# Linear attention, expert routing and a gated MLP on one core: loads from two queues, score products in one group, a separate tile for token ids

## The chip, the core and the metric

The kernel runs on one core of a Trainium2 chip. The core has a matrix engine (PE, TensorE; its weight loads are shown as PEld), two elementwise engines (DVE, VectorE, and ACT, ScalarE), a general engine (POOL, GpSimd) and an engine that only issues transfers (SP, SyncE). ACT and POOL can issue transfers too; an instruction that issues one stands in its engine's own stream and waits there for its semaphores. Sixteen DMA engines move the data. The metric is the time of one execution in microseconds; a run's time is compared as a median.

## The reference

Three stages follow each other. `B, H, S, D = 4, 8, 768, 48`, so there are 3072 tokens of 384 features.

```
f = sigmoid(f_logit)
for t in range(S):
    state = f[:, :, t, :, None] * state + outer(k[:, :, t], v[:, :, t])
    y[:, :, t] = q[:, :, t] @ state
x = y as (3072, 384)
expert_idx = argmax(normalized(x) @ normalized(expert_emb).T / tau); gate_w = softmax value of it
x[mask_e] = gate_w * (relu(x[mask_e] @ w1[e]) @ w2[e])          # 8 experts, 384 -> 1024 -> 384
out = ((x @ w_a) * (x @ w_b)) @ w_out                            # 384 -> 1536 -> 384
```

## The kernel before

**Attention (L119 to L619).** The sequence is cut into 24 groups `g` (6 chunks of 128 tokens, 4 batches each, `B` = 4). For each group `load_a` (L168) brings q, k and the gate logits (`qkf`, two halves of 48 partitions, 288 KB each; the partition rows between them are zeroed by a load of `zgap`), and `load_b` (L175) brings v in two layouts (`vx`, `vT`). `prep_f` (L183) makes the gate on ACT, `prep_s` (L189) makes on DVE a running product and its inverse by two scans and from them the tiles `kt` and `qc`. The function `pe(g)` (L303) is one round of PE: score products `pp` of group g+2 (`p_part`, L246, four parts), the products of group g with the state (`inter`) and with its masked scores (`intra`), the key-value part of group g+1 (`kv_part`), and the state update (`u_part`). PE also multiplies constants (`warm_up`, L298, tile `wp`): 22 before the first round, 5, 4 and 2 in the rounds, 24 at the end. `NKEEP` (L47) gives 4 for rounds 0 to 3 and 2 for rounds 4 to 22. `evac` (L334) takes a group's result to `yx` (8 buffers). A `route` generator, advanced by `tick` between the other DVE instructions, computes the expert, the gate and the slot of each token; `scale_row` (L427) writes the gated rows and the token's number into `xr` (3 buffers), and `scatter_row` sends them to the table `slots` in DRAM, by an indirect transfer that POOL issues.

**Experts (L622 to L878).** 64 steps `s` (8 experts, 8 slices of the hidden width). For each expert `rows_load` (L728) brings up to 448 token rows into the one tile `rows`; `x_turn` transposes them (PE, `pt`) in steps 3 to 5 of the expert before; `h_mm` and `y_part` are the products. `ids_store` (L738) writes the token numbers, column `DM` of `rows`, to `idlist` in DRAM, and the next `rows_load` follows it on SP and overwrites `rows`. The weights come through two `raw` buffers and are split into two parts by ACT, POOL and DVE (`job_load` L653, `job_run` L666).

**Gated MLP (L881 to L972).** 72 steps of products; the results are scattered to the output by the ids.

The order of each engine's instructions is the order of the Python code: nothing reorders them. A transfer from SP or ACT takes one of eight completion semaphores (DMAHW0 to DMAHW7 below), shared by both queues; it waits until the transfer that held that semaphore before has landed. `bufs` of a tile says how many buffers it goes round.

Of the kernel before, what the change touches and what calls it, by code (L numbers as in the profile page):

```python
# [6 lines left out]
F32 = mybir.dt.float32  # L7
# [3 lines left out]
ACTF = mybir.ActivationFunctionType  # L11
# [5 lines left out]
B, H, S, D = 4, 8, 768, 48  # L17
NT, DM, NE, FF, FF2 = B * S, H * D, 8, 1024, 1536
L = 128
NCH = S // L  # L20
NP = H // 2
HP = 112
QP = 128
VW = D + NE
KC = DM // 128
CAP = 448
RW = 388
# [16 lines left out]
NWARM2 = 0  # L44
NWARM3 = 24
ZR = 192
NKEEP = (4, 2)  # L47


def build(tc, I, out, dbg=None):  # L50
    nc = tc.nc
    V, A, T, G, SP = nc.vector, nc.scalar, nc.tensor, nc.gpsimd, nc.sync
# [66 lines left out]
    with tc.manual_schedule():  # L119
# [4 lines left out]
        ob_p = actx.enter_context(tc.tile_pool(name="ob", bufs=1))  # L124
        x_p = actx.enter_context(tc.tile_pool(name="x", bufs=12))
# [7 lines left out]
        NG = NCH * B  # L133
# [8 lines left out]
        en_bd = ob_p.tile([128, KC, H * NE], F32, name="en_bd")  # L142
# [6 lines left out]
        qkf_t = [ob_p.tile([QP, 3, NP, L], F32, name=f"qkf{i}") for i in range(5)]  # L149
# [18 lines left out]
        def load_a(g):  # L168
            if g < NG:
                qkf = qkf_t[g % 5]  # L170
                for i in range(2):
                    SP.dma_start(out=qkf[64 * i:64 * i + D], in_=I["qkf"][g, i])
                st[g] = dict(qkf=qkf)

        def load_b(g):  # L175
            if g < NG:
                vx = in_p.tile([128, H, VW], F32, tag="vx", name="vx", bufs=4)
                SP.dma_start(out=vx, in_=I["vx"][g])
                vT = in_p.tile([128, KC, L], F32, tag="vT", name="vT")
                SP.dma_start(out=vT, in_=I["vT"][g])  # L180
                st[g].update(vx=vx, vT=vT)
# [60 lines left out]
        def p_open(g):  # L242
            if g < NG:
                st[g]["ps"] = [ps_p.tile([128, NP, L], F32, tag="pp", name="pp") for i in range(2)]

        def p_part(g, p):  # L246
            if g >= NG:
                return
            d = st[g]
            for i in range(2):  # L250
                r = slice(64 * i, 64 * i + 64)
                T.matmul(out=d["ps"][i][:, p], lhsT=d["kt"][r, p], rhs=d["qc"][r, p], start=True, stop=True)
# [36 lines left out]
        def intra(g, ps):  # L289
            if g < 0:  # L290
                return
            d = st[g]
            for p in ps:
                for i in range(2):
                    T.matmul(out=d["y"][:, 2 * p + i], lhsT=d["pm"][i][:, p], rhs=d["vx"][:, 2 * p + i],
                             start=(g < B and p == 0 and i == 0), stop=True, skip_group_check=True)

        def warm_up(n):  # L298
            wp = ps_kv.tile([128, 512], F32, tag="kv", name="wp")
            for i in range(n):  # L300
                T.matmul(out=wp, lhsT=ones, rhs=warm, start=(i == 0), stop=(i == n - 1))

        def pe(g):  # L303
            n = g + 2
            if 0 <= g < NG - 1:
                warm_up(NKEEP[g >= B])
            p_open(n)
            p_part(n, 0)
            if g == -1:
                warm_up(NWARM1)  # L310
            p_part(n, 1)
            p_part(n, 2)
            inter(g)
            intra(g, (0,))
            p_part(n, 3)
            kv_part(g + 1)
            it[0] += 0.5
            tick(2)
            p_mask(n)
            intra(g, (1, 2, 3))  # L320
            u_part(g)
            return st.pop(g)["y"] if g >= 0 else None
# [10 lines left out]

        def evac(g, y, rd):  # L334
            i = len(rd["x"])
            yx = x_p.tile([128, H, VW], F32, tag="yx", name="yx", bufs=8)
            A.activation(out=yx, in_=y, func=ACTF.Copy)
            junk = x_p.tile([128, H, D], BF16, tag="junk", name="junk", bufs=1)
            A.activation(out=junk, in_=yx[:, :, 0:D], func=ACTF.Square, accum_out=rd["ssq"][:, i:i + 1])
            late.append(lambda: V.tensor_reduce(out=rd["lg"][:, i], in_=yx[:, :, D:VW].rearrange("p h e -> p e h"),  # L340
                                                axis=AX.X, op=ALU.add))
            rd["x"].append((g, yx))
# [82 lines left out]
        scq, scaled = [], []  # L425

        def scale_row():  # L427
            if scq:
                if len(scaled) == 3:
                    scatter_row()  # L430
                g, yx, gate, posi = scq.pop(0)
                xr = x_p.tile([128, RW], F32, tag="xr", name="xr", bufs=3)
                c, b = divmod(g, B)
                G.iota(out=xr[:, DM:RW], pattern=[[0, RW - DM]], base=b * S + c * L, channel_multiplier=1,
                       allow_small_or_imprecise_dtypes=True)
                A.activation(out=xr[:, 0:DM].rearrange("p (h e) -> p h e", h=H), in_=yx[:, :, 0:D], func=ACTF.Copy,
                             scale=gate)
                scaled.append((xr, posi))
# [35 lines left out]
                    except StopIteration:  # L474
                        bg.pop(0)

        for i in range(5):
            for r in (48, 112):
                SP.dma_start(out=qkf_t[i][r:r + 16], in_=I["zgap"].rearrange("p (a b c) -> p a b c", a=3, b=NP))
            if i < 2:  # L480
                load_a(i)
            if i == 0:
                SP.dma_start(out=en_bd, in_=I["embbd"])
                tau = ob_p.tile([128, 1], F32, name="tau")
                SP.dma_start(out=tau, in_=I["tau"].to_broadcast([128, 1]))
                load_b(0)
        V.memset(half, 0.5)
        V.memset(ones, 1.0)
        V.memset(warm, 0.0)
        A.activation(out=half, in_=half, func=ACTF.Tanh, scale=0.0, bias=0.0)  # L490
        V.memset(half, 0.5)
        onesf = raw0[:, 512:640]
# [22 lines left out]
        prep_s(0)  # L515
        V.tensor_reduce(out=en, in_=pe_ps.rearrange("p h e -> p e h"), axis=AX.X, op=ALU.add)
        G.tensor_tensor(out=en, in0=en, in1=half, op=ALU.pow)
        load_a(2)
        load_b(1)
        load_a(3)  # L520
        load_b(2)
        load_a(4)
        prep_f(2)
        prep_s(1)
        V.tensor_scalar(out=en, in0=en, scalar1=1e-6, scalar2=tau, op0=ALU.add, op1=ALU.mult)
# [98 lines left out]
        ectx = ExitStack()  # L624
        ap = ectx.enter_context(tc.tile_pool(name="acts", bufs=4))
        hp = ectx.enter_context(tc.tile_pool(name="hid", bufs=2))
        sp = ectx.enter_context(tc.tile_pool(name="solo", bufs=1))
        yT = [sp.tile([128, NT + CAP], F32, name=f"yT{k}") for k in range(KC)]
        rows = sp.tile([128, 4, RW], F32, name="rows")
        idr = sp.tile([24, 128], F32, name="idr")  # L630
# [107 lines left out]
        def ids_store(e):  # L738
            if e == 0:
                dst = idlist[0, 0:CAP]  # L740
            else:
                rs = SP.value_load(off_i[0:1, e:e + 1], **off_range(e))  # L742
                dst = idlist[0, bass.ds(rs, CAP)]
            SP.dma_start(out=dst.rearrange("(p j) -> p j", j=4), in_=rows[0:HP, :, DM])

        def x_turn(e, k):
            if e >= NE:
# [104 lines left out]
        for s in range(NE * FJ):  # L852
            e, j = divmod(s, FJ)
# [13 lines left out]
            if s == IDS + 4:  # L867
# [5 lines left out]
                ids = sp.tile([128, NT // 128], F32, name="ids")  # L873
# [300 lines left out]
```

## Time and profile before

| what | value |
|---|---|
| runs, us | 935.67, 937.55, 947.85 (median 937.55) |
| the profiled execution, us | 946.78, with a span of 945.1 from first to last instruction |
| mean granted clock of PE | 0.967 of 2.4 GHz |
| busy: PE, PEld, DVE, ACT, POOL | 95%, 83%, 44%, 36%, 24% of the span |

The profile is one execution. Times in its rows are microseconds from the first instruction unless marked ns. A matrix product of 32-bit operands shows as two records, so a group of six products reads x12. Ends of products are modelled, and neighbours overlap, so lengths are best taken from start to start. The granted clock is 1.00 at 2.4 GHz and 0.50 at 1.2 GHz. Attention lies from 0 to about 212 us, the experts from 217 to about 480, the gated MLP behind that.

### The profile page before, as it was taken

What the parts mean: (1) busy time and instruction counts of PE and PEld (TensorE: products, weight loads), DVE (VectorE), ACT (ScalarE), POOL (GpSimd) and SP (SyncE); (2) the same over time, 40 slices, a digit from 0 to 9 for tenths busy, and PEclk for the clock granted to TensorE, in tenths of its full rate; (3) what the DMA queues carried; (4) which work ended last, traced back from release to release, by engine and by line L of the source; (5) the groups of instructions that cost most, each with busy time, mean ns of one, the idle gap of its engine ahead of it and who ended that gap; (6) DMA issues with size and microseconds to landing.
All of it is one profiled execution on the core that took longest, in us unless ns stands there. A gap on an engine that the chain in (4) does not pass through costs nothing.

```text
span 945.1 us, 12533 instructions
## 1 busy us (share of the span) xinstructions
PE 895.5 (95%) x4908; PEld 781.4 (83%) x4931; DVE 417.0 (44%) x789; ACT 336.1 (36%) x601; POOL 226.7 (24%) x221
## 2 busy tenths in 40 slices
PE   5999999968989998999999899999999999999996
PEld 2788888847978897898988788888888888888885
DVE  5577787742434442343678852222322322222222
ACT  2365666533444353344434421212212222122221
POOL 2123344556253353354222211001001001001001
PEclk8599999979999999999999999999999999999999
DMA  9777877324254545535533300000000000000001
GB/s 177 184 198 197 212 201 190 124 110 126 69 157 115 138 146 146 146 102 163 102 101 101 101 1 34 0 1 34 1 1 34 1 1 34 0 1 34 1 1 37
DMA packets 42806, 83.15 MB, mean 88 GB/s; under 512 B 7532, under 2 KB 24900, under 8 KB 42740
## 3 DMA queue, kind: packets, MB, share of 16 engines
q1 hardware_dynamic: 39668, 72.78, 29.4%
q0 software_dynamic: 3072, 9.49, 2.8%
q8 instruction: 41, 0.67, 0.3%
q14 instruction: 25, 0.20, 0.1%
HBM read 70.36 MB, written 11.90 MB: 87 GB/s over the span
## 4 chain that ended last, share of the span: by engine, by line
issue 48%; DMA 12%; POOL 7%; PE 5%; SPq 1%; DVE 1%; POOLq 0%; ACT 0%; DVEq 0%; ACTq 0%
DMA idlist<-rows 5%; DMA raw<-moe_w 5%; POOL w L672 3%; PE po L812 2%; POOL w L690 2%; POOL out L937 2%; DMA rows<-slots 1%; PE ph L759 1%; PE ph L760 1%; PE ph L761 1%; SPq L742 0%; SPq L663 0%; PE pt L752 0%; DVE ct L681 0%; SPq L732 0%
## 5 line engine op out<-in xcount | busy, mean ns | idle before, releaser
L761 PE MATMUL pa<-a,w 128*128 128x512 f32 (+1 forms) x438 | 170.5, 389 | 0.0
L760 PE MATMUL pa<-a,w 128*128 128x512 f32 (+1 forms) x438 | 170.4, 389 | 0.0
L759 PE MATMUL pa<-a,w 128*128 128x512 f32 (+1 forms) x438 | 169.2, 386 | 0.0
L910 DVE TENSOR_TENSOR rows<-rows,pa 128x512 f32<-128x512 f32 (+1 forms) x73 | 49.6, 680 | 242.7 <-PE pa L761 242.7
L937 POOL DMA_INDIRECT out<-yT,idx x24 | 23.4, 976 | 363.7 <-ACT yT L935 358.3
L672 POOL TENSOR_TENSOR w<-raw,w 128x512 fp32r<-128x512 f32 x56 | 84.9, 1541 | 73.8 <-ACT w L669 73.6
L906 ACT ACTIVATE rows<-pa 128x512 f32<-128x512 f32 (+1 forms) x73 | 43.1, 591 | 163.9 <-PE pa L761 163.7
L925 PE MATMUL pq<-w,gl 128*128 128x384 f32 x288 | 98.1, 341 | 2.1 <-DVE gl L912 2.0
L923 PE MATMUL pq<-w,gh 128*128 128x384 f32 x288 | 97.6, 339 | 0.8 <-ACT gh L911 0.8
L924 PE MATMUL pq<-w,gh 128*128 128x384 f32 x288 | 97.3, 338 | 0.0
L911 ACT ACTIVATE gh<-rows 128x512 fp32r<-128x512 f32 (+1 forms) x73 | 45.6, 625 | 144.6 <-DVE rows L910 144.6
L761 PEld LDWEIGHTS pa<-a,w 128*128 128x128 f32 x438 | 82.2, 188 | 16.9
L760 PEld LDWEIGHTS pa<-a,w 128*128 128x128 f32 x438 | 82.3, 188 | 15.4
L759 PEld LDWEIGHTS pa<-a,w 128*128 128x128 f32 x438 | 82.4, 188 | 15.1
L812 PE MATMUL po<-hh,w 128*128 128x448 f32 x384 | 93.8, 381 | 0.0
L912 DVE TENSOR_TENSOR gl<-rows,gh 128x512 fp32r<-128x512 f32 (+1 forms) x73 | 60.1, 823 | 52.1 <-ACT gh L911 52.1
L812 PEld LDWEIGHTS po<-hh,w 128*128 128x128 f32 x384 | 72.8, 195 | 6.2 <-ACT hh L781 0.4
L759 PE MATMUL ph<-a,w 128*128 128x448 f32 x192 | 71.0, 370 | 0.0
L760 PE MATMUL ph<-a,w 128*128 128x448 f32 x192 | 70.6, 367 | 0.0
L761 PE MATMUL ph<-a,w 128*128 128x448 f32 x192 | 70.4, 367 | 0.0
L781 ACT ACTIVATE hh<-ph 128x448 fp32r<-128x448 f32 x64 | 34.8, 544 | 99.7 <-PE ph L761 99.5
L782 DVE SCALAR_TENSOR_TENSOR hl<-ph,hh 128x448 fp32r<-128x448 f32 x64 | 39.8, 622 | 64.9 <-ACT hh L781 64.6
(158 smaller groups left out, 1419.2 us busy)
## 6 DMA issues: line engine op xcount, KB each, us to landing
raw<-moe_w SPq DMA_DIRECT2D x32, 768.0 KB, 5.7
qkf<-qkf SPq DMA_DIRECT2D x48, 288.0 KB, 6.4
vx<-vx SPq DMA_DIRECT2D x24, 224.0 KB, 2.6
rows<-slots SPq DMA_DIRECT2D x7, 679.0 KB, 6.3
vT<-vT SPq DMA_DIRECT2D x24, 192.0 KB, 2.7
raw<-moe_w_a SPq DMA_DIRECT2D x6, 768.0 KB, 4.5
raw<-moe_w_b SPq DMA_DIRECT2D x6, 768.0 KB, 4.5
raw<-moe_w_out SPq DMA_DIRECT2D x6, 768.0 KB, 4.6
```

What stands on the lines that cost most here:

```text
L672: (G if i < NPOOL else V).tensor_tensor(out=wt[:, 1, f], in0=raw[:, f], in1=wt[:, 0, f].bitcast(F32), op=ALU.subtract)
L759: T.matmul(out=out, lhsT=wh, rhs=xh, start=first, stop=False)
L760: T.matmul(out=out, lhsT=wl, rhs=xh, start=False, stop=False)
L761: T.matmul(out=out, lhsT=wh, rhs=xl, start=False, stop=last)
L812: T.matmul(out=OS[e][k], lhsT=w[:, j % 4, k * 128:(k + 1) * 128], rhs=x, start=(j == 0 and w is wh and x is hh), stop=(j == FJ - 1 and x i ...
L906: A.activation(out=ab[:, r], in_=pa, func=ACTF.Copy)
L910: V.tensor_tensor(out=ab[:, r], in0=ab[:, r], in1=pp[1], op=ALU.mult)
L911: A.activation(out=gh[:, r], in_=ab[:, r], func=ACTF.Copy)
L912: V.tensor_tensor(out=gl[:, r], in0=ab[:, r], in1=gh[:, r].bitcast(F32), op=ALU.subtract)
L923: T.matmul(out=q, lhsT=gh[:, c], rhs=wh[:, f % 4], start=(f == 0), stop=False)
L924: T.matmul(out=q, lhsT=gh[:, c], rhs=wl[:, f % 4], start=False, stop=False)
L925: T.matmul(out=q, lhsT=gl[:, c], rhs=wh[:, f % 4], start=False, stop=(f == F2J - 1))
```

## The change

- `load_a` issues the first half of `qkf` from SP and the second from ACT, in every round. Of the ten `zgap` loads the two of the first buffer stay (one from each queue); the other four buffers are cleared whole by DVE (two) and POOL (two). The loads of the first groups are all issued ahead of the first ACT instruction.
- `pe` computes the four score parts of a group in one go, ahead of `inter` and `intra`, and multiplies constants in rounds 0 to 3 alone (4 each).
- `yx` has 7 buffers in place of 8, `xr` 4 in place of 3.
- `ids_store` copies the ids with ACT to a tile of their own (two buffers) and stores from that.

```diff
--- before.py
+++ after.py
@@ -44,7 +44,7 @@
 NWARM2 = 0
 NWARM3 = 24
 ZR = 192
-NKEEP = (4, 2)
+NKEEP = 4
 
 
 def build(tc, I, out, dbg=None):
@@ -168,8 +168,8 @@
         def load_a(g):
             if g < NG:
                 qkf = qkf_t[g % 5]
-                for i in range(2):
-                    SP.dma_start(out=qkf[64 * i:64 * i + D], in_=I["qkf"][g, i])
+                for i, eng in enumerate((SP, A)):
+                    eng.dma_start(out=qkf[64 * i:64 * i + D], in_=I["qkf"][g, i])
                 st[g] = dict(qkf=qkf)
 
         def load_b(g):
@@ -302,17 +302,15 @@
 
         def pe(g):
             n = g + 2
-            if 0 <= g < NG - 1:
-                warm_up(NKEEP[g >= B])
+            if 0 <= g < B:
+                warm_up(NKEEP)
             p_open(n)
-            p_part(n, 0)
+            for p in range(NP):
+                p_part(n, p)
             if g == -1:
                 warm_up(NWARM1)
-            p_part(n, 1)
-            p_part(n, 2)
             inter(g)
             intra(g, (0,))
-            p_part(n, 3)
             kv_part(g + 1)
             it[0] += 0.5
             tick(2)
@@ -333,7 +331,7 @@
 
         def evac(g, y, rd):
             i = len(rd["x"])
-            yx = x_p.tile([128, H, VW], F32, tag="yx", name="yx", bufs=8)
+            yx = x_p.tile([128, H, VW], F32, tag="yx", name="yx", bufs=7)
             A.activation(out=yx, in_=y, func=ACTF.Copy)
             junk = x_p.tile([128, H, D], BF16, tag="junk", name="junk", bufs=1)
             A.activation(out=junk, in_=yx[:, :, 0:D], func=ACTF.Square, accum_out=rd["ssq"][:, i:i + 1])
@@ -426,10 +424,10 @@
 
         def scale_row():
             if scq:
-                if len(scaled) == 3:
+                if len(scaled) == 4:
                     scatter_row()
                 g, yx, gate, posi = scq.pop(0)
-                xr = x_p.tile([128, RW], F32, tag="xr", name="xr", bufs=3)
+                xr = x_p.tile([128, RW], F32, tag="xr", name="xr", bufs=4)
                 c, b = divmod(g, B)
                 G.iota(out=xr[:, DM:RW], pattern=[[0, RW - DM]], base=b * S + c * L, channel_multiplier=1,
                        allow_small_or_imprecise_dtypes=True)
@@ -474,19 +472,26 @@
                     except StopIteration:
                         bg.pop(0)
 
-        for i in range(5):
-            for r in (48, 112):
-                SP.dma_start(out=qkf_t[i][r:r + 16], in_=I["zgap"].rearrange("p (a b c) -> p a b c", a=3, b=NP))
-            if i < 2:
-                load_a(i)
-            if i == 0:
-                SP.dma_start(out=en_bd, in_=I["embbd"])
-                tau = ob_p.tile([128, 1], F32, name="tau")
-                SP.dma_start(out=tau, in_=I["tau"].to_broadcast([128, 1]))
-                load_b(0)
+        load_a(0)
+        for r, eng in ((48, SP), (112, A)):
+            eng.dma_start(out=qkf_t[0][r:r + 16], in_=I["zgap"].rearrange("p (a b c) -> p a b c", a=3, b=NP))
+        SP.dma_start(out=en_bd, in_=I["embbd"])
+        tau = ob_p.tile([128, 1], F32, name="tau")
         V.memset(half, 0.5)
         V.memset(ones, 1.0)
         V.memset(warm, 0.0)
+        V.memset(qkf_t[1], 0.0)
+        V.memset(qkf_t[2], 0.0)
+        for i in (3, 4):
+            G.memset(qkf_t[i], 0.0)
+        load_a(1)
+        SP.dma_start(out=tau, in_=I["tau"].to_broadcast([128, 1]))
+        load_b(0)
+        load_a(2)
+        load_b(1)
+        load_a(3)
+        load_b(2)
+        load_a(4)
         A.activation(out=half, in_=half, func=ACTF.Tanh, scale=0.0, bias=0.0)
         V.memset(half, 0.5)
         onesf = raw0[:, 512:640]
@@ -515,11 +520,6 @@
         prep_s(0)
         V.tensor_reduce(out=en, in_=pe_ps.rearrange("p h e -> p e h"), axis=AX.X, op=ALU.add)
         G.tensor_tensor(out=en, in0=en, in1=half, op=ALU.pow)
-        load_a(2)
-        load_b(1)
-        load_a(3)
-        load_b(2)
-        load_a(4)
         prep_f(2)
         prep_s(1)
         V.tensor_scalar(out=en, in0=en, scalar1=1e-6, scalar2=tau, op0=ALU.add, op1=ALU.mult)
@@ -625,6 +625,7 @@
         ap = ectx.enter_context(tc.tile_pool(name="acts", bufs=4))
         hp = ectx.enter_context(tc.tile_pool(name="hid", bufs=2))
         sp = ectx.enter_context(tc.tile_pool(name="solo", bufs=1))
+        idp = ectx.enter_context(tc.tile_pool(name="idp", bufs=2))
         yT = [sp.tile([128, NT + CAP], F32, name=f"yT{k}") for k in range(KC)]
         rows = sp.tile([128, 4, RW], F32, name="rows")
         idr = sp.tile([24, 128], F32, name="idr")
@@ -741,7 +742,9 @@
             else:
                 rs = SP.value_load(off_i[0:1, e:e + 1], **off_range(e))
                 dst = idlist[0, bass.ds(rs, CAP)]
-            SP.dma_start(out=dst.rearrange("(p j) -> p j", j=4), in_=rows[0:HP, :, DM])
+            ids = idp.tile([HP, 4], F32, tag="ids", name="ids")
+            A.activation(out=ids, in_=rows[0:HP, :, DM], func=ACTF.Copy)
+            SP.dma_start(out=dst.rearrange("(p j) -> p j", j=4), in_=ids)
 
         def x_turn(e, k):
             if e >= NE:
```

Three places show what this does to the order of the instructions. The names are the program's, with a buffer's number.

The first is ACT at the start of the program, before (the semaphores that an instruction waits for stand in brackets):

```order
L490 ACT_TABLE_LOAD
L490 ACTIVATE half<-half 128x8 [waits DVE_49]
L186 ACTIVATE F_129<-qkf_131 128x4x128 [waits DMAHW2_49,DMAHW1_49,DMAHW3_49,DMAHW0_49,DVE_49]
L187 ACTIVATE F_129<-F_129 128x4x128 [waits Activation_49]
L186 ACTIVATE F_130<-qkf_132 128x4x128 [waits DMAHW2_49,DMAHW1_49,DMAHW3_49,DMAHW0_49,DVE_49]
```

and with the change:

```order
L172 DMA qkf_131<-qkf 48x1536
L477 DMA qkf_131<-zgap 16x1536
L172 DMA qkf_132<-qkf 48x1536 [waits DVE_49]
L172 DMA qkf_133<-qkf 48x1536 [waits DVE_49]
L172 DMA qkf_134<-qkf 48x1536 [waits DMAHW4_49,Pool_49]
L172 DMA qkf_135<-qkf 48x1536 [waits DMAHW6_49,Pool_49]
L495 ACT_TABLE_LOAD
L495 ACTIVATE half<-half 128x8
L186 ACTIVATE F_129<-qkf_131 128x4x128 [waits DMAHW2_49,DMAHW1_49,DMAHW3_49,DMAHW0_49,DVE_49]
```

Six transfers now stand ahead of the table load; two of them wait for DVE, and the last two for the landing of earlier transfers (semaphores 4 and 6, which the two halves of the second `qkf` hold) and for POOL.

The second is PE at the boundary of two rounds in the middle of the attention, before:

```order
L275 MATMUL u_ps<-vx,ktT 112x112 x4
L301 LDWEIGHTS ones
L301 MATMUL wp<-warm,ones 128x512
L301 LDWEIGHTS ones
L301 MATMUL wp<-warm,ones 128x512
L252 MATMUL pp<-qc,kt 128x128 x6
L286 MATMUL y<-S_125,qc 128x112 x4
L295 MATMUL y<-vx,pm 128x56 x2
L252 MATMUL pp<-qc,kt 128x128 x2
L233 MATMUL kv<-en_bd,vT 128x64 x3
L236 MATMUL kv<-ident,kt 128x112 x4
L295 MATMUL y<-vx,pm 128x56 x6
```

and with the change:

```order
L275 MATMUL u_ps<-vx,ktT 112x112 x4
L252 MATMUL pp<-qc,kt 128x128 x8
L286 MATMUL y<-S_127,qc 128x112 x4
L295 MATMUL y<-vx,pm 128x56 x2
L233 MATMUL kv<-en_bd,vT 128x64 x3
L236 MATMUL kv<-ident,kt 128x112 x4
L295 MATMUL y<-vx,pm 128x56 x6
L273 MATMUL u_ps<-S_127,ident 112x448
```

The two constant products and their weight loads are gone, and the eight score products stand together.

The third is SP in an expert, before:

```order
L742 TENSOR_LOAD off_i
L742 ISA x2
L744 REGISTER_ALU
L744 DMA idlist<-rows 448x1x1 [waits DMAHW7_49]
L732 DMA rows<-slots 112x1552 [waits DMAHW4_49,PE_49]
L663 DMA raw<-moe_w 128x4x384 [waits DMAHW2_49,Pool_49]
```

and with the change:

```order
L743 TENSOR_LOAD off_i
L743 ISA x2
L747 REGISTER_ALU
L747 DMA idlist<-ids 112x4 [waits DMAHW6_49,Activation_49]
L733 DMA rows<-slots 112x1552 [waits DMAHW7_49,PE_49]
L664 DMA raw<-moe_w 128x4x384 [waits DMAHW2_49,Pool_49]
```

The store takes its ids from `ids`, waits for ACT, and writes 112 runs of 4 numbers in place of 448 single ones; the load of `rows` behind it waits for PE's transposes and for one earlier transfer, and no longer for the store.

## Rows read from the trace of the kernel before

**Rows 1.** Stretches: from:to, length; busy PE, PEld, DVE, ACT, POOL; clock, DMA share, GB/s.
```profile
10.00:15.00 5.00, 4.68 (x27) 2.06 (x25) 3.46 (x7) 0.63 (x1) 1.36 (x1) 0.73 1.06 165
19.50:43.40 23.90, 19.91 (x87) 14.74 (x89) 12.82 (x24) 10.22 (x21) 4.26 (x6) 0.50 0.81 179
45.00:190.00 145.00, 142.27 (x1242) 122.72 (x1262) 112.46 (x277) 90.28 (x211) 55.17 (x79) 1.00 0.70 189
127.40:134.70 7.30, 7.15 (x65) 6.17 (x66) 6.38 (x16) 4.55 (x11) 2.37 (x5) 1.00 0.75 222
260.00:270.00 10.00, 6.87 (x29) 5.96 (x28) 2.35 (x3) 2.12 (x3) 4.52 (x3) 0.83 0.71 221
```

**Rows 2.** Timeline of PE at the start: start, length, what [idle before <-releaser].
```profile
19.94 0.79 PE L252 MATMUL pp<-qc,kt 64*128 64x128 f32 x2 [3.46 <-DVE qc L216]
23.31 0.79 PE L252 MATMUL pp<-qc,kt 64*128 64x128 f32 x2 [2.58 <-ACT pm L262]
...
38.12 2.67 PE L295 MATMUL y<-vx,pm 128*128 128x56 f32 x12
```

**Rows 3.** Timeline of DVE at the start.
```profile
2.39 0.07 DVE L491 MEMSET half<- 128x8 f32 x1 [1.00 <-ACT half L490]
...
4.49 0.43 DVE L503 MEMSET u_ps<- 128x448 f32 x1
...
9.22 1.23 DVE L200 TENSOR_TENSOR_SCAN Bt<-F,pat 128x516 f32<-128x516 f32 x1 [0.84 <-ACT F L187]
...
33.03 1.23 DVE L200 TENSOR_TENSOR_SCAN Bt<-F,pat 128x516 f32<-128x516 f32 x1 [1.41 <-ACT F L187]
...
41.41 0.27 DVE L340 TENSOR_REDUCE lg<-yx 128x8 f32<-128x64 f32 x1 [7.14 <-ACT yx L337]
```

**Rows 4.** Waits of DVE from 9 to 35 us: total, times, longest.
```profile
DVE Bt L200 <- ACT F L187: 6.5, 4, 2.1
```

**Rows 5.** Timeline of ACT and of SP's queue at the start.
```profile
0.82 1.28 ACT L490 ACT_TABLE_LOAD   x1 [0.82 <-PEq L1167]
...
1.73 0.89 SPq L172 DMA_DIRECT2D qkf<-qkf  x2
```

**Rows 6.** DMA issues from 0 to 44 us: KB each, median us to landing.
```profile
qkf<-qkf SPq DMA_DIRECT2D x15, 288.0 KB, 7.3
...
qkf<-zgap SPq DMA_DIRECT2D x10, 96.0 KB, 6.7
```

**Rows 7.** Timeline of PE in one round, from 112 to 118 us.
```profile
112.62 0.38 PE L301 MATMUL wp<-warm,ones 128*128 128x512 bf16 x1
113.15 0.94 PE L252 MATMUL pp<-qc,kt 64*128 64x128 f32 x12
114.02 1.15 PE L286 MATMUL y<-S,qc 112*128 112x112 f32 x8
...
115.49 0.49 PE L252 MATMUL pp<-qc,kt 64*128 64x128 f32 x4
115.91 0.88 PE L233 MATMUL kv<-en_bd,vT 128*128 128x64 f32 x6
...
117.02 1.46 PE L295 MATMUL y<-vx,pm 128*128 128x56 f32 x12
```

**Rows 8.** Timeline of DVE in the round of 127 us.
```profile
127.78 0.69 DVE L114 TENSOR_TENSOR w<-raw,w 128x512 fp32r<-128x512 f32 x1 [0.90 <-ACT w L106]
```

**Rows 9.** Timeline of ACT, then of PE, at the end of the attention.
```profile
196.72 0.62 ACT L436 ACTIVATE xr<-yx,gate 128x384 f32<-128x384 f32 x1 [2.76 <-DMA slots<-xr,posi]
...
197.54 3.63 PE L295 MATMUL y<-vx,pm 128*128 128x56 f32 x16 [2.93 <-POOL xr L434]
```

**Rows 10.** Waits of PE in the experts, 225 to 480 us.
```profile
PE pt L752 <- DMA rows<-slots: 13.2, 6, 3.1
```

**Rows 11.** Waits of SP's queue from 205 to 480 us.
```profile
SPq L663 <- DVE w L672: 69.9, 19, 10.0
SPq L732 <- DMA idlist<-rows: 62.4, 7, 9.8
```

## The prediction

> **What bounds the kernel.** I read the busy times by stretch first, then the timelines of PE and DVE at the start, the transfers, one round, the tail, and last the waits of the experts. In the middle of the attention, 45 to 190 us, PE is busy 142.27 of 145 us at a granted clock of 1.00, while DVE has 112.46 and ACT 90.28 [rows 1]: what PE no longer does there is time. PE is not the bound in three places: the start, where the clock is at 0.50 from 19.5 to 43.4 us; a wait at the end of the attention [rows 9]; and six waits for token rows in the experts, 13.2 us together [rows 10], around which the clock falls too (0.83 from 260 to 270 us) [rows 1].
>
> All sums are made against the profiled execution: 946.78 us, its span of 945.1 and 1.7 around it. That lies 9.2 above the median of the runs, 937.55.
>
> **A. The start.** Second queue: one queue already fills the DMA engines (share 1.06 at 165 GB/s from 10 to 15 us [rows 1]), so two issuers add no rate. What helps is that 8 of the 10 `zgap` loads go: 8 x 96 KB [rows 6] at 165 GB/s is 4.8 us of transfer. In their place stand memsets of 1536 columns: by 0.43 us for 448 columns [rows 3] each costs 1.5, so 2.9 on DVE and, if POOL is no slower, as much there, while the loads run: nothing.
>
> But ACT now issues six transfers ahead of its table load, 0.45 us each (0.89 for two [rows 5]), and the last two wait until the halves of the second `qkf` have landed. Those are issued behind DVE's memsets, at about 3 us; with 7.3 us to landing [rows 6] that is 10.3. Two issues (0.9), the table load (1.28 [rows 5]) and a small instruction bring ACT to 13. DVE's second memset of `half` waits for that; from there to the end of its start-up, which ran from 2.39 to 4.92, is 2.5 [rows 3]. The first scan of `Bt` so starts near 16, in place of 9.22: 6.7 late. Behind it the waits for `F` should go, since by then four groups have landed: of 6.5 us in four waits [rows 4], the 0.84 ahead of the first scan [rows 3] lies before that point, and 5.7 are regained. DVE's preparation ends 1.0 late, taken as 1.2.
>
> What follows hangs on the clock. Before, `lg` started at 41.41 after DVE had waited 7.14 for PE's first round [rows 3], because PE ran at 0.50 there, after idles of 3.46 and 2.58 between its score products [rows 2]: twelve records of `y` took 2.67 there and take 1.46 later [rows 2, 7], a factor of 1.83. The 19.91 us busy from 19.5 to 43.4 [rows 1] are 10.9 at the higher clock. With DVE's waits gone PE's inputs come close together, and I expect the higher clock to last into the first round. Then `lg` waits little: 41.41 - 7.14 + 1.2 = 35.5, with a rest of a wait 35.8, a gain of **5.6**. Bounds: 7.1 (no lateness), and a loss of 1.2 if PE stays slow and preparation is late.
>
> **B. The rounds.** From one `wp` to the score products is 0.53 us (112.62 to 113.15 [rows 7]), for the two constant products. Score products in one go: 12 records take 0.87 (113.15 to 114.02) and 4 take 0.42 (115.49 to 115.91) [rows 7]; 16 in one stretch at 0.87 / 12 each are 1.16, so 0.13 less. Together 0.66 a round, of which I take 0.6, as PE was idle for 2% of the stretch. Rounds 4 to 22 are 19: **11.4**. Bounds: 12.5 if all of it counts, and 3.8 (0.2 a round) if DVE takes over early. In rounds 0 to 3 only the grouping counts: 4 x 0.13 = **0.5**. The cover that must hold is DVE: 6.38 busy of a round of 7.30 [rows 1], against a new round of 6.7. ACT gets one transfer issue of 0.45 a round beside 4.55 of 7.30 busy [rows 1]: hidden, though it stands ahead of ACT's work of that round. `yx` with one buffer less: a buffer is freed by the ACT copy to `xr`, which the order puts ahead of the later `yx`; nothing.
>
> A rule speaks against B. The row: the clock is 1.00 through 45 to 190, with constants in every round [rows 1]; none shows it without. The Trainium skill, "TensorE: Matmul & The Clock Gate", section "A second HAM failure mode: psum-queue depth-cycling", says that short idles of PE between groups of products can be frequent enough that its clock keeps changing between two levels. By the row B is 11.4 gained; by the rule it is the fourth rival's loss.
>
> **C. The tail.** ACT waits 2.76 us for the scatter that holds the oldest `xr`, and PE waits 2.93 in front of its last products [rows 9]. A fourth buffer takes that wait away: **2.8**. Bounds: nothing (the next wait, for the slots, takes its place), and 4.4 if the clock also stays up for the last products (3.63 us [rows 9] at 1.83 times less would be 1.6 saved).
>
> **D. Experts.** The load of `rows` followed the store of 448 single numbers and waited 62.4 us in 7 waits, 8.9 each [rows 11]. With the ids in their own tile it waits for PE's transposes alone and lands some 9 us earlier, while PE's longest wait for it is 3.1: all six go, **13.2** [rows 10]. I see three of them that also bring the clock down; in the one of 260 to 270 us PE's 0.83 means a third of the stretch at half speed, 3.4 us, of which half is lost: 1.7, three times **5.1**. Bounds: 0 if something else is late, and 23.4 if all of the 3.4 is lost each time. The eight small copies on ACT, about 0.2 each by estimate, lie beside ACT's idle (2.12 busy of 10 [rows 1]). What is late next: the weights; SP waits 69.9 us in 19 waits for a free `raw` buffer, behind DVE's splitting [rows 11], but that queue then works ahead of PE.
>
> **The sum.** -5.6 - 11.4 - 0.5 - 2.8 - 18.3 = -38.6; 946.78 - 38.6 = 908.2. If the start of the median run had not been slow, the sum from it is 937.55 + 1.2 - 33.0 = 905.8. I predict **908**.
>
> **Rivals.**
> 1. *The start stays at 0.50.* For: the first product still waits for a DVE chain that begins 6.7 later, and PE has only short constants before it. Against: the waits between are gone. A turns from -5.6 to +1.2: 915. Chance 0.10.
> 2. *DVE becomes the bound in the rounds with routing work.* In the round of 127.4 it is busy 6.38 and waits 0.90 for ACT's `w` [rows 1, 8], 7.28 of 7.30: if that wait is a fixed part of the round, PE's 0.6 is lost in some 12 rounds, 7.2: 915. Against: the wait comes from splitting weights, which can shift. Chance 0.15.
> 3. *The expert waits return*, since the weights are late or the store still holds the queue. Against: 9 us of room where 3.1 are wanted. With half of D gone 917, with all 926. Chance 0.06.
> 4. *Other side: the clock falls in the rounds.* The constants lay at a round's border, where PE could otherwise be idle; without them it may wait for `qc` or for the state, and at 0.50 a round of 6.6 costs 1.83 times that, 12.1: 5.5 more each. PE then falls behind and is busy throughout, which speaks for its return to 1.00, so it changes to and fro. With half of 19 rounds slow that is +52: 960. From 5.4 slow rounds on nothing is left of the gain against the median (908.2 + 29.4), and from 8.8 on it is slower by 2%. Against: grouping makes PE's work denser. Chance 0.06.
>
> The forecast has 0.63. A measurement here tells 2%: faster means below 918.8, slower above 956.3. Forecast, rivals 1 and 2 and a little of 3 lie below 918.8, less a mishap of two rivals together: faster 0.81. Most of 3, such pairs, and a few slow rounds are the same: 0.13; slower 0.06. The range: at the low end the terms at their better bounds, 946.78 - 7.1 - 12.5 - 0.5 - 4.4 - 23.4 = 899; at the high end rivals 1 and 2 together, 922. What is outside (rival 4, the worse of 3) is under 2 in 10.
>
> **What would show it.** In the profile after: A, a first scan near 16, no idle above 1 us between PE's first score products, a clock of 1.00 before 43 us, `lg` near 36. B, rounds of 6.6 to 6.7 from 60 to 185 at 1.00 and no `wp` there; rounds still of 7.28 with DVE's waits on ACT gone would mean rival 2, a clock under 1.00 rival 4. C, no ACT idle in front of the last `xr`. D, `pt` no longer waits for `rows`, SP's wait for the store gone, and 1.00 from 225 to 480. The prediction is wrong if the rounds lose their clock, or if PE's stalls in the experts come back under another name.

## The result, and the profile after

The changed kernel takes 910.82 us (median of four runs, 903.85 to 912.31) against 937.22 for the kernel before (four runs as well); the recorded ratio of the runs is 0.968, 95% interval 0.9592 to 0.9768, while the two medians by themselves give 0.972. The forecast was 908 in a range of 899 to 922. Single executions of one kernel differ with PE's mean clock: of the changed kernel's four the shortest, 903.85, has 0.984 and the others 0.972 or 0.973, and of experiment 1's four below two take about 919 at 0.980 or 0.981 and two 928.7 at 0.970 or 0.972. The profiled execution took 909.4, its span went from 945.1 to 907.7 us: 37.4 less, where the sum of the terms said 38.6. The terms themselves did not all come out so, and the single execution profiled before is not the median; the experiments below separate the two.

Starts in the traces (us), of every kernel that this document speaks of. "kv 4" and "kv 20" are PE's first product of `kv` for groups 4 and 20, so 16 whole rounds lie between them; "pt" is PE's first transpose of the experts, "pa" its first weight load in the gated MLP.

| kernel | lg | kv 4 | kv 20 | pt | pa | kv 4 to kv 20, a round | kv 20 to pt | pt to pa |
|---|---|---|---|---|---|---|---|---|
| before | 41.41 | 57.76 | 174.83 | 216.87 | 480.5 | 7.32 | 42.0 | 263.6 |
| changed | 35.09 | 48.90 | 153.64 | 199.03 | 443.1 | 6.55 | 45.4 | 244.1 |
| 1 ids' tile alone | 36.18 | 50.95 | 168.02 | 210.12 | 453.0 | 7.32 | 42.1 | 242.9 |
| 2 constants back | 35.46 | 48.28 | 160.00 | 198.39 | 444.0 | 6.98 | 38.4 | 245.6 |
| 3 DVE relieved | 35.47 | 48.28 | 153.02 | 189.87 | 434.0 | 6.55 | 36.9 | 244.1 |
| 4 wait filled | 35.49 | 48.30 | 153.04 | 192.23 | 436.7 | 6.55 | 39.2 | 244.5 |
| 5 old start | 34.57 | 48.38 | 153.12 | 199.03 | 443.2 | 6.55 | 45.9 | 244.2 |
| 6 no grouping | 35.44 | 50.22 | 160.29 | 205.63 | 449.5 | 6.88 | 45.3 | 243.9 |
| 7 table first | 28.71 | 43.24 | 148.58 | 193.69 | 437.8 | 6.58 | 45.1 | 244.1 |
| 8 three xr | 35.59 | 49.34 | 154.08 | 199.82 | 443.4 | 6.55 | 45.7 | 243.6 |
| 9 no ids' tile | 35.49 | 49.31 | 154.05 | 199.16 | 459.9 | 6.55 | 45.1 | 260.7 |
| 10 both | 28.48 | 43.06 | 148.74 | 185.80 | 430.3 | 6.61 | 37.1 | 244.5 |
| 11 both, 35 constants | 28.02 | 42.52 | 148.62 | 186.45 | 429.4 | 6.63 | 37.8 | 243.0 |

From the first two lines: the kernel gains 8.9 us up to kv 4, 12.3 in 16 rounds, loses 3.4 from kv 20 to the experts, and gains 19.6 in the experts; behind that nothing differs.

**Start.** Timeline of DVE in the changed kernel, answering [rows 3]:

```profile
13.01 0.07 DVE L496 MEMSET half<- 128x8 f32 x1 [8.40 <-ACT half L495]
...
15.70 1.22 DVE L200 TENSOR_TENSOR_SCAN Bt<-F,pat 128x516 f32<-128x516 f32 x1
...
35.09 0.27 DVE L338 TENSOR_REDUCE lg<-yx 128x8 f32<-128x64 f32 x1
```

and of ACT, answering [rows 5]:

```profile
3.03 8.38 ACTq L172 DMA_DIRECT2D qkf<-qkf  x4
11.44 1.28 ACT L495 ACT_TABLE_LOAD   x1 [11.44 <-DMA qkf<-qkf]
```

ACT stands in its transfers until 11.44, DVE waits 8.40 for it (the idle in front of its memset at 13.01), and the first scan starts at 15.70 in place of 9.22. No scan waits for a gate after that, and `lg` follows at 35.09.

**Rounds and tail.** Stretches of the changed kernel (from:to, length, busy PE, PEld, DVE, ACT, POOL, clock, DMA share, GB/s), answering [rows 1]:

```profile
20.00:25.00 5.00, 4.95 (x31) 2.47 (x32) 4.83 (x10) 2.44 (x5) 3.83 (x3) 0.79 1.07 260
25.00:30.00 5.00, 4.20 (x35) 2.58 (x33) 4.90 (x9) 1.82 (x6) 0.46 (x2) 1.00 0.53 105
...
60.00:150.00 90.00, 90.00 (x838) 81.41 (x835) 82.54 (x200) 62.75 (x147) 41.26 (x54) 1.00 0.89 222
...
160.00:165.00 5.00, 3.04 (x34) 2.77 (x35) 4.87 (x15) 3.89 (x9) 3.47 (x5) 1.00 0.11 43
165.00:170.00 5.00, 5.00 (x32) 4.88 (x28) 0.68 (x4) 0.44 (x3) 1.96 (x2) 0.55 0.73 240
170.00:175.00 5.00, 5.00 (x25) 5.00 (x25) 2.05 (x13) 2.20 (x6) 2.29 (x7) 0.50 0.00 0
...
204.00:443.00 239.00, 238.98 (x1220) 220.15 (x1219) 112.79 (x171) 106.76 (x157) 99.64 (x64) 1.00 0.46 140
```

In the rounds PE is now busy in every microsecond (90.00 of 90) and the clock holds, without constants from round 4 on. But DVE is nearly full too: 82.54 of 90, where [rows 1] had 112.46 of 145. At 165 us the clock falls to half. Timeline of PE there:

```profile
160.48 1.50 PE L295 MATMUL y<-vx,pm 128*128 128x56 f32 x12
163.94 0.18 PE L377 MATMUL rk<-oh,tri 128*128 128x32 bf16 x1 [1.96 <-DVE oh L374]
...
164.35 1.16 PE L252 MATMUL pp<-qc,kt 64*128 64x128 f32 x16
165.44 2.02 PE L286 MATMUL y<-S,qc 112*128 112x112 f32 x8
...
169.31 2.75 PE L295 MATMUL y<-vx,pm 128*128 128x56 f32 x12
```

PE waits 1.96 for DVE's `oh`, and from 165.44 on every product takes nearly twice its time (`y` x12 2.75, where it took 1.50 nine microseconds before). Rounds 20 to 23 have no state update, so PE's part of them is short and DVE's is not; with constants DVE had the slack to be there in time (experiment 2).

**Experts.** Waits of SP's queue in the changed kernel, 195 to 480 us, answering [rows 11]:

```profile
SPq L664 <- POOL w L691: 124.9, 13, 13.8
SPq L664 <- POOL w L673: 66.8, 28, 2.8
SPq L664 <- DVE w L673: 47.5, 21, 10.0
SPq L747 <- ACT ids L746: 8.8, 1, 8.8
SPq L733 <- PE ph L763: 0.9, 5, 0.2
```

The load of `rows` (L733) no longer waits for the store. SP now waits for weight buffers, 239 us in all, and PE for nothing: 238.98 busy of 239, clock 1.00 in the stretch above; the six waits of [rows 10] have no row any more.

### The profile page after: what moved, and what is told of

It is laid out like the page before. It is cut to its first block, busy times and chain, and to the rows that moved or that the text cites. A ratio compares the mean times of both kernels' runs of the same rounds, so it can differ in the third digit from the quotient of the medians.

```text
span 907.7 us, 12520 instructions
## 1 busy us (share of the span) xinstructions
PE 873.2 (96%) x4888; PEld 772.0 (85%) x4893; DVE 428.2 (47%) x791; ACT 336.8 (37%) x609; POOL 237.5 (26%) x223
## 5 line engine op out<-in xcount | busy, mean ns | idle before, releaser
L815 PE MATMUL po<-hh,w 128*128 128x448 f32 x384 | 90.1, 370 | 0.0
L815 PEld LDWEIGHTS po<-hh,w 128*128 128x128 f32 x384 | 70.5, 188 | 5.4 <-ACT hh L784 0.4
```

The source lines that it names most:

```text
L815: T.matmul(out=OS[e][k], lhsT=w[:, j % 4, k * 128:(k + 1) * 128], rhs=x, start=(j == 0 and w is wh and x is hh), stop=(j == FJ - 1 and x i ...
```

## The experiments

Eleven kernels, each timed against the kernel before. Ratios stand with their 95% intervals; the changed kernel has 0.968 (0.9592 to 0.9768). The kernel before, measured again beside them, had a median of 938.4 us with experiments 1 to 4, 941.61 with 5 to 8 and 937.94 with 9 to 11, so a difference of some 4 us between medians of different sets says nothing by itself; the starts in the table go beside them.

**1. The ids' tile alone**, in the kernel before:

```diff
+        idp = ectx.enter_context(tc.tile_pool(name="idp", bufs=2))
...
-            SP.dma_start(out=dst.rearrange("(p j) -> p j", j=4), in_=rows[0:HP, :, DM])
+            ids = idp.tile([HP, 4], F32, tag="ids", name="ids")
+            A.activation(out=ids, in_=rows[0:HP, :, DM], func=ACTF.Copy)
+            SP.dma_start(out=dst.rearrange("(p j) -> p j", j=4), in_=ids)
```

> The kernel before with the ids' own tile alone. My account (the wait for the store goes, and with it the stretches at the lower clock in the experts): PE's six waits for rows are gone, 1.00 from 225 to 480 us, 18 to 20 us less than the kernel before, ratio 0.980. Rival (only the waits count, the clock loss is small): 13 us, ratio 0.986.

924.23 us, ratio 0.9871 (0.9803 to 0.994), the rival's value; but the trace has the experts in 242.9 us against 263.6, which is my account. The interval takes in the rival's 0.986 and ends just above my 0.980; the profiled execution is the shortest of the four (918.84). A stretch of its start and that of its experts:

```profile
30.00:36.00 6.00, 6.00 (x55) 5.04 (x55) 2.83 (x3) 3.94 (x9) 2.39 (x4) 1.00 1.08 279
...
215.00:453.00 238.00, 237.97 (x1216) 219.30 (x1215) 112.87 (x171) 106.78 (x157) 99.80 (x65) 1.00 0.46 140
```

The start was not touched, yet its clock is 1.00 from 30 us, where the profiled run of the kernel before had 0.50 to 43.4 [rows 1], and `lg` comes at 36.18 against 41.41. The slow start of that one execution is not a constant of the program.

**2. Constants back** in rounds 4 to 22, the grouping kept:

```diff
-            if 0 <= g < B:
-                warm_up(NKEEP)
+            if 0 <= g < NG - 1:
+                warm_up(NKEEP if g < B else 2)
```

> The changed kernel with two constant products ahead of the scores in rounds 4 to 22 again. Theory 1 (without constants DVE has no slack, is late at the last rounds, and PE's wait for it brings the clock down): rounds 0.53 longer, 9 to 10 us; the wait of 1.96 for oh gone and the clock at 1.00 to the last rounds, 5 to 7 us back; in all +3 to +5 against the changed kernel, 913 to 916. Rival (the clock at the end of the attention falls whatever DVE does): +10, about 920.

910.25 us, ratio 0.9704 (0.9655 to 0.9753): no later than the changed kernel. A round takes 6.98, 0.44 longer, 7.0 us over 16 rounds; from kv 20 to the experts it is 7.0 shorter (38.4 against 45.4), with constants in three rounds of that too. Stretches of it, and PE at the place of the wait:

```profile
60.00:150.00 90.00, 88.25 (x802) 77.78 (x813) 75.39 (x185) 58.73 (x137) 37.26 (x50) 1.00 0.84 211
...
165.00:170.00 5.00, 4.48 (x43) 3.85 (x40) 4.45 (x12) 2.30 (x7) 3.36 (x6) 1.00 0.35 120
```

```profile
169.29 0.18 PE L377 MATMUL rk<-oh,tri 128*128 128x32 bf16 x1 [0.52 <-DVE oh L374]
```

DVE has 75.39 of 90 busy, the wait is 0.52, and the clock stays. Taking the constants out of 19 rounds so earned nothing in the end: what the rounds gave, the tail took. I had expected +3 to +5: a round's constants cost less than the 0.53 that I had said, and the clock's return was worth more.

**3. DVE relieved**: the last four weight splits moved behind the attention.

```diff
-            if 9 <= g < LATE_G:
+            if 9 <= g < 17:
...
-        w_load()
         while wstate["lo"] < 12:
             w_hi()
             w_lo(V)
+        w_load()
+        w_load()
```

> The changed kernel with the last four of twelve weight splits (0.69 to 0.88 us each on DVE, in rounds 17 to 20) moved behind the attention, where DVE and ACT are idle. Theory 1: DVE's oh is no longer late, PE's wait of 1.96 shrinks under 0.5, the clock stays 1.00 through 165 to 180, the first transpose of the experts comes at 192 to 194 in place of 199.0; 903 to 906. Rival (without constants the last rounds are too thin to keep the clock): it falls before 180 all the same, gain under 2 us.

900.26 us, ratio 0.9616 (0.9563 to 0.9669), better than expected. PE at the same place, and its arrival in the experts:

```profile
159.86 1.50 PE L295 MATMUL y<-vx,pm 128*128 128x56 f32 x12
161.19 0.18 PE L377 MATMUL rk<-oh,tri 128*128 128x32 bf16 x1
...
164.76 1.50 PE L295 MATMUL y<-vx,pm 128*128 128x56 f32 x12
...
176.93 0.19 PE L377 MATMUL rk<-oh,tri 128*128 128x16 bf16 x1 [3.62 <-DVE oh L374]
...
189.87 1.61 PE L755 MATMUL pt<-ident,rows 112*128 112x112 f32 x8 [2.51 <-DMA rows<-slots]
```

No wait and no fall of the clock at that place (`y` x12 keeps 1.50), the experts 9.2 us earlier, 8.5 of it behind kv 20. The clock falls later, at about 177 us (0.69 on the mean from 175 to 180), where PE has come to the end of its rounds and waits 3.62 for DVE's chain of small instructions; that is before the 180 that I had set. But the last full products run ahead of it at 1.00, and the rival, last rounds too thin for the clock without constants, with a gain under 2 us, is out.

**4. The wait filled** with constants, DVE as late as before:

```diff
+            if i0 == 19:
+                warm_up(9)
             ps = ps_r.tile([128, B, NE], F32, tag="r", name="rk")[:, 0:nb]
```

> The changed kernel with nine constant products (0.21 us each) in front of the ranks of the group of round 19, which fill the 1.96 us that PE waits there for DVE. Theory 2 (it is PE's idleness, not DVE's lateness as such, that costs): the ranks start as late as before, 163.9, but the clock stays 1.00 after it, 4 to 6 us less than the changed kernel, 904 to 907. Rival (DVE stays behind, PE idles at the next place and the clock falls there): within 1 us of the changed kernel, 910.

902.6 us, ratio 0.963 (0.9578 to 0.9682).

```profile
161.22 2.11 PE L301 MATMUL wp<-warm,ones 128*128 128x512 bf16 x8
163.35 0.18 PE L379 MATMUL rk<-oh,tri 128*128 128x32 bf16 x1
...
166.91 1.50 PE L295 MATMUL y<-vx,pm 128*128 128x56 f32 x12
```

The ranks start 10.3 us behind kv 20, as in the changed kernel: nothing is gained at the wait itself. But `y` stays at 1.50, and kv 20 to pt takes 39.2 in place of 45.4. The price was the clock behind the idle, as theory 2 had it; 3 shows that DVE's lateness made the idle, and is worth 2.3 more, by the medians and by kv 20 to pt alike, though the two intervals overlap.

**5. The old start**: one queue, ten `zgap` loads, the loads in their old places, no clearing (the old blocks of L172 and L477 to L488 put back).

```diff
-                for i, eng in enumerate((SP, A)):
-                    eng.dma_start(out=qkf[64 * i:64 * i + D], in_=I["qkf"][g, i])
+                for i in range(2):
+                    SP.dma_start(out=qkf[64 * i:64 * i + D], in_=I["qkf"][g, i])
```

> The changed kernel with the loads of the kernel before: one queue, ten zgap loads, the table load first, no clearing of buffers. By the prediction's part A with a slow start: first scan near 9.2, lg near 41, +5.6, 915 to 917. Rival (in most runs the old start already reaches the higher clock before 30 us, as in the run with the ids' own tile alone, where lg stood at 36.18 against 35.09 here): lg at 35.5 to 36.5, +1 to +2, 911 to 913, with single runs some 6 us longer.

910.29 us, ratio 0.969 (0.9611 to 0.9768); one run of four was 917.89. The rival: `lg` stands at 34.57, half a microsecond *earlier* than with the new start.

```profile
20.00:25.00 5.00, 2.46 (x16) 1.91 (x16) 2.82 (x6) 2.23 (x4) 1.73 (x2) 0.50 1.04 219
25.00:30.00 5.00, 4.20 (x25) 2.23 (x25) 4.90 (x9) 2.90 (x6) 0.83 (x1) 0.90 1.07 254
30.00:36.00 6.00, 5.95 (x61) 5.22 (x62) 3.95 (x8) 4.74 (x11) 2.90 (x4) 1.00 1.07 261
```

Issued as they are in the changed kernel, the two queues and the memsets gain nothing; experiment 7 shows what they are worth otherwise.

**6. No grouping**: the score parts in their old places, without constants.

```diff
-            for p in range(NP):
-                p_part(n, p)
+            p_part(n, 0)
             if g == -1:
                 warm_up(NWARM1)
+            p_part(n, 1)
+            p_part(n, 2)
             inter(g)
             intra(g, (0,))
+            p_part(n, 3)
             kv_part(g + 1)
```

> The changed kernel with the four score parts in their old places, the constants of rounds 4 to 22 left out. By the prediction the grouping is worth 0.13 a round: rounds 6.64 in place of 6.51, 22 rounds, +2.9, of which some goes into DVE's lateness at the end: 912 to 914. Rival (the gap between groups is hidden by weight loads): rounds 6.51 to 6.55, within 1 us.

916.79 us, ratio 0.9729 (0.9654 to 0.9803). A round takes 6.88: grouping is worth 0.33, not 0.13, and pa comes 6.4 us later than in the changed kernel, where I had expected 2.9. PE without grouping:

```profile
108.96 0.94 PE L252 MATMUL pp<-qc,kt 64*128 64x128 f32 x12
109.83 1.15 PE L286 MATMUL y<-S,qc 112*128 112x112 f32 x8
110.81 0.56 PE L295 MATMUL y<-vx,pm 128*128 128x56 f32 x4
111.30 0.49 PE L252 MATMUL pp<-qc,kt 64*128 64x128 f32 x4
111.72 0.88 PE L233 MATMUL kv<-en_bd,vT 128*128 128x64 f32 x6
112.44 0.55 PE L236 MATMUL kv<-ident,kt 112*128 112x112 f32 x4
```

and in the changed kernel:

```profile
118.28 1.16 PE L252 MATMUL pp<-qc,kt 64*128 64x128 f32 x16
119.38 1.15 PE L286 MATMUL y<-S,qc 112*128 112x112 f32 x8
120.36 0.56 PE L295 MATMUL y<-vx,pm 128*128 128x56 f32 x4
120.76 0.84 PE L233 MATMUL kv<-en_bd,vT 128*128 128x64 f32 x6
121.43 0.55 PE L236 MATMUL kv<-ident,kt 112*128 112x112 f32 x4
```

From start to start: scores 0.87 + 0.42 against 1.10; the `y` ahead of the lone part 0.49 against 0.40; `kv` behind it 0.72 against 0.67. The change of kind costs its neighbours as well, 0.33 together.

**7. The table load first**, and the waiting transfers behind ACT's first two gates:

```diff
+        A.activation(out=half, in_=half, func=ACTF.Tanh, scale=0.0, bias=0.0)
         load_a(1)
...
         load_b(1)
-        load_a(3)
-        load_b(2)
-        load_a(4)
-        A.activation(out=half, in_=half, func=ACTF.Tanh, scale=0.0, bias=0.0)
...
         prep_f(0)
         prep_f(1)
+        load_a(3)
+        load_b(2)
+        load_a(4)
```

> The changed kernel with ACT's table load behind its first two transfers, and the loads of the fourth and fifth group behind ACT's first two gates. If ACT's wait for the second group's landing (11.4 us) is what delays the start: first scan near 9.5 in place of 15.7, lg at 30 to 32 in place of 35.09, 3 to 5 us less, 906 to 908. Rival (the loads themselves bound the start, the DMA engines being full until 25 us): first scan early, but the third and fourth scans wait for their gates and lg stays within 1.5 of 35.

904.56 us, ratio 0.96 (0.9529 to 0.9671). DVE:

```profile
9.12 1.23 DVE L200 TENSOR_TENSOR_SCAN Bt<-F,pat 128x516 f32<-128x516 f32 x1 [0.79 <-ACT F L187]
...
28.71 0.27 DVE L338 TENSOR_REDUCE lg<-yx 128x8 f32<-128x64 f32 x1 [0.18 <-ACT yx L335]
...
34.41 1.23 DVE L200 TENSOR_TENSOR_SCAN Bt<-F,pat 128x516 f32<-128x516 f32 x1 [1.62 <-ACT F L187]
```

The first scan comes 6.6 earlier and `lg` 6.4. So the loads did not bound the start; ACT, held in its own transfers, did. A later scan waits 1.62 for its gate, and by kv 4 the lead is 5.7; what bounds the start then was not tested. Beside experiment 5, which also has the table load first, this kernel has the new loads in place of the old, and its `lg` is 5.9 earlier (28.71 against 34.57) and its kv 4 5.1: the new loads do gain, once ACT does not stand in them. Which part of them it is, the second queue, the `zgap` loads that went, the order, or the clock that comes up sooner behind them (1.00 from 20 us here, 0.50 from 20 to 25 there), no run separates.

**8. Three `xr` buffers**:

```diff
-                if len(scaled) == 4:
+                if len(scaled) == 3:
...
-                xr = x_p.tile([128, RW], F32, tag="xr", name="xr", bufs=4)
+                xr = x_p.tile([128, RW], F32, tag="xr", name="xr", bufs=3)
```

> The changed kernel with three xr buffers in place of four. By the prediction's part C: ACT waits about 2.8 for the scatter in front of the late yx, and the first transpose of the experts comes 2 to 3 us later, 201 to 202 in place of 199.0; 912 to 914. Rival (the end is set by DVE's chain and by PE at the lower clock, and the wait lies beside them): under 0.7 us.

911.82 us, ratio 0.9686 (0.962 to 0.9753); kv 20 to pt 45.7 against 45.4. ACT does wait for the scatter again:

```profile
179.52 0.61 ACT L434 ACTIVATE xr<-yx,gate 128x384 f32<-128x384 f32 x1 [2.61 <-DMA slots<-xr,posi]
```

PE has no wait for it. In this tail, with PE at half its clock, the buffer is worth 0.3, the rival's value. In a tail at full clock it wasn't tried.

**9. No ids' tile**: experiment 1's edit taken out of the changed kernel.

> The changed kernel with the store of the ids from column 384 of rows again. If the ids' own tile is worth what the profiles show between the first transpose and the first product of the gated MLP (263.6 us before, 244.1 with the change): +19 to +20, 930. If it is worth what the runs of the ids' own tile alone showed in their median (ratio 0.9871): +12 to +14, 923 to 925.

926.3 us, ratio 0.9889 (0.9841 to 0.9937), between the two and nearer to the second. The experts take 260.7 against 244.1, so the tile is worth 16.7 us here and 20.7 in the traces of 1. PE's waits differ from those of before, and are 8.9 us together where they were 13.2:

```profile
PE po L812 <- ACT yT L830: 5.9, 3, 2.9
PE pt L752 <- DMA rows<-slots: 3.0, 1, 3.0
```

**10 and 11. Both improvements** (3 and 7 together), and the same with `NWARM3` 35 in place of 24.

> The changed kernel with both improvements: the last four weight splits behind the attention, and the table load ahead of the waiting transfers. If they are independent, 10.6 and 6.3 us below the changed kernel, 893 to 895; lg near 28.7, clock 1.00 from 20 us to 172 us. Rival (DVE, full in the rounds, gives part of the early start back): 897 to 900.

> The same with 35 constant products in place of 24 ahead of the experts, 11 x 0.21 = 2.3 us, into the idle of 2.5 us that PE had there before its first transposes. If that idle is what brings the clock to 0.66 in the five microseconds after it: first products at 0.37 in place of 0.57 to 0.72 us, 1.5 to 2 us less than without. Rival (the clock falls for another reason): no difference, or +0.5 where the constants run past the landing.

895.77 us, ratio 0.9543 (0.9501 to 0.9585), and 894.87, ratio 0.9542 (0.95 to 0.9583). They add up but for 1 to 2 us: `lg` is 6.6 earlier than in the changed kernel, but a round takes 6.61 in place of 6.55. The 11 constants do keep the clock. Without them, then with them:

```profile
185.80 1.41 PE L755 MATMUL pt<-ident,rows 112*128 112x112 f32 x8 [2.40 <-DMA rows<-slots]
187.06 0.74 PE L762 MATMUL ph<-a,w 128*128 128x448 f32 x1
```

```profile
186.45 0.93 PE L755 MATMUL pt<-ident,rows 112*128 112x112 f32 x8
187.68 0.47 PE L762 MATMUL ph<-a,w 128*128 128x448 f32 x1 [0.30 <-ACT a L758]
```

Products take 0.47 in place of 0.74, and pt to pa is 1.5 shorter; but kv 20 to pt is 0.8 longer, since PE now comes to its transposes from constants and not from a wait, and the runs do not tell the two kernels apart. Some constants fewer might keep both; that was not tried.

## Why the prediction came out

The total was right; three of its terms were not. Between the two profiles the start, the rounds and the tail gave 17.8 us where A, B and C said 20.3, and the experts 19.6 where D said 18.3. That the number came out as near against the median was in part luck: A counted a slow start that the median does not have, and B and C promised more than they gave.

**A, the start: right for the trace, wrong for the cause.** The chain was as written: ACT at 11.44, the first scan at 15.70 (near 16 was said), no waits for gates after it, the higher clock from 25 us, `lg` at 35.09 (35.8). But the step "PE ran at 0.50 there" took one execution for the program. Experiments 1 and 5 have the old start with the clock at 1.00 from 30 us, and `lg` at 36.18 and 34.57; and of 25 later executions of the kernel before only four have a mean clock about as low as the profiled one's 0.967 (0.968 or less). Where the old start is not slow, nothing of the 5.6 us is the change's. The second sum, from the median with a start that is not slow, had the better premise, though its 905.8 lies further from 910.82 than 908.2 does, since B and C gave less. A gain was there to be had in the new loads (5.9 at `lg`, experiment 7 beside 5); ACT, held in its transfers, gave it back.

**B, the rounds: the size right, the parts exchanged, and the clock forgotten at the end.** Together 0.77 a round was measured where 0.66 was worked out. Constants gave 0.44, not 0.53, since the state update ahead of them takes 0.88 to the next start where it took 0.78 ahead of constants; grouping 0.33, not 0.13, since I priced the scores alone (1.16 in one go, where they took 1.10) and not what a change of kind costs `y` and `kv` beside them. The failing step is "the cover that must hold is DVE": the cover was checked against a mean round, 6.38 against 6.7, and did hold there. It did not in rounds 20 to 23, where PE's part is shorter and DVE's is not. Rival 2 (DVE becomes the bound) and rival 4 (the clock falls without constants) so came true together in one place: DVE took no round, but its lateness made an idle of 1.96, and the clock fell behind it for the rest of the attention. Experiments 4, 2 and 3 put that at 6.2, 7.0 and 8.5 us between kv 20 and pt, about what the constants had cost in 16 rounds (7.0), so that B gave its grouping alone, some 6.6 of 11.9. All twelve executions of these three kernels have a mean clock of 0.980 or more, against 0.972 or 0.973 in three of the changed kernel's four; the fourth, 903.85 at 0.984, seems to have been spared most of the fall, but it has no trace.

By the page "TensorE: Matmul & The Clock Gate" of the Trainium skill, section "A second HAM failure mode: psum-queue depth-cycling", short idles between groups of products made the clock change to and fro in another kernel. That didn't happen here: it is 1.00 from 25 to 165 us, from round 4 on without constants. One idle near 2 us at the end did the harm, and the clock did not come back in the next 15 us, though PE is counted busy in all of them.

**C, the tail: wrong.** 2.8 was forecast; experiment 8 shows 0.3. The wait for `xr` was real [rows 9]. But in the changed kernel's tail PE runs at half its clock and comes to its last products later: with three buffers ACT waits 2.61 for the scatter again, and PE does not. What sets the end there is, by the timelines, PE at half its clock and DVE's chain of small instructions; no run takes the two apart.

**D, the experts: right.** 18.3 forecast; 19.6 between the profiles, 16.7 and 20.7 in experiments 9 and 1. The wait for the store went, the weights that SP now waits for are early enough, and the clock is 1.00 from 204 to 443 us.

**The sum by experiments**, from the traces: constants +7.0 - 7.0, grouping 5.3 in 16 rounds and 1.3 before them, `xr` 0.3, ids' tile 16.7 to 20.7, start 0: 23.6 to 27.6 us, against 26.4 between the medians. The 37.4 between the two profiles holds 6.8 more of the slow start of the one execution (57.76 against 50.95 at kv 4 in experiment 1).

What stays open: why the old start recovers its clock at 26 to 30 us in two traces and at 43 in one, with the same loads; and how much of the ids' tile's 16.7 to 20.7 us is clock and how much waiting in a typical run, since the median of experiment 1 shows 14, and that of 9 lies 15.5 above the changed kernel's.

## What to carry to other kernels

Filler work that keeps a clock up is worth what the worst idle that it covers would cost: here it could go from the full rounds, while the last rounds needed it, or better the slack that it had given the late engine. Check a cover in the round where the bounding engine has least to do, not in the mean round. And before a term is built on a slow stretch of one profiled execution, ask what that stretch is in the median: a sum from both points costs a line, and here the one from the median had the right premise for the start.

An engine that issues transfers stands in them. Two transfers that wait for a landing held ACT for 8 us, and behind ACT DVE; a transfer that must wait belongs on a queue whose engine has nothing else to do, or behind that engine's first work (the second was run, in experiment 7; the first was not).

## What the runs showed of the hardware

- A group of two small 32-bit products (four records) between others costs more than its own 0.42 us: its neighbours took 0.09 and 0.05 longer, and eight products in one go took 1.10 where six and two took 1.29 (experiment 6 and the changed kernel).
- After an idle of 1.96 us PE's clock was at half from 165 us on, and three stretches with PE busy 5.00 of 5 us, to 180 us, did not bring it back. The same idle filled with constants left it at 1.00 until about 177 us, where PE waits again (experiment 4).
- DVE's scan of 516 columns, 1.23 us in the kernel before, took up to 1.66 in the changed kernel's rounds, with a median of 1.23. No experiment looked for the cause.
